# A third of eight ff pairs by seven products in the second product, with sums of one piece a row

## The chip, the cores and the metric

The kernel runs on one core of a Trainium2 chip. The metric is device time in microseconds; the median of three runs of the kernel before is 1011.67 us (1010.93 to 1014.6).

## The reference

A gated linear scan over 6080 time steps of 2 sequences with 256 channels gives 12160 tokens; each then passes a feed-forward layer of 2048 hidden units with a gate of its own:

```python
sig = 1.0 / (1.0 + np.exp(-f_logit))
f = lower_bound + (1.0 - lower_bound) * sig
for t in range(S):
    h = f[:, t] * h + (1.0 - f)[:, t] * x[:, t]
    y[:, t] = h
h = y.reshape(B * S, D) @ w_in            # 12160 x 256 by 256 x 2048
g = h * np.clip(h + 3.0, 0.0, 6.0) / 6.0
out = (g @ w_out).astype(np.float32)      # by 2048 x 256
```

## The kernel before

**Tiles.** Channels, hidden units and outputs lie on the partitions, tokens along the rows. Tokens are cut into 24 runs (`token_runs`): 20 of 512 columns and 4 of 480, alternately of sequence 0 and 1. The 2048 hidden units are 16 ff blocks of 128. Every float32 operand is split into a high part (rounded to the matmul's format, on ACT) and a low part (the rest, on DVE), and a product of two blocks is three matmuls: high by high, high by low, low by high. `split` is this pair of instructions (lines 406 to 415).

**Stages.** The first four runs are computed directly (`direct`, line 575). From then on runs go in ten pairs. `prep_pair` loads the gate input (`ft`) and x (`xt`) of both runs, scans them and builds the operands of the first product; sums of operands are made by DMAs that POOL issues and that add into their destination (`add_into`, line 246). For each of 8 pairs of ff blocks, `quad` makes the 2 x 2 block product (two ff blocks by two token runs) with seven block products instead of eight (`seven`, matmuls on line 620) and applies the gate (`gate`: ACT line 481, DVE line 483).

**Second product.** For most ff pairs it is plain: `mm2`, eight block products of three matmuls (line 512). For the first GROUP = 2 ff pairs of a run pair, in nine of the ten run pairs, `chain` uses seven products here too. It needs seven operands, each split: b11, b21, b22 are gated blocks as they are, t1, t3, t2 and t4 are sums, made in place in w11 and w12 by four POOL DMAs. Both ff pairs lie in one buffer of two blocks a row, so one DMA or one split serves both. The weight sums are made once by `prep_s2`.

**What sets the order.** A planner (`ordered`) lists every instruction as a job with a cost, needs and a due time that comes from PE's own order, and writes the five engines' programs in the order it plans. Each engine then runs its program in that order and waits where something is not ready. In PE's order products of the quads alternate with a fill from `queue` (plain second products and the steps of `chain`); FILLS says how many. `Ring` is a set of buffers used in turn; a new use waits for all users of the old one. `SCRATCH` is the space in SBUF, per partition, where descriptors of POOL's DMAs are kept. Buffers are placed `[P, 2, BANK]`: with 480 columns the second block begins 32 columns behind the end of the first.

Of the kernel before, what the change touches and what calls it, by code (L numbers as in the profile page):

```python
# [20 lines left out]
GROUP = 2  # L21
FILLS = ((2, 3, 3),) * 7 + ((2, 2, 2),)
# [39 lines left out]
class Ring:  # L62


    def __init__(self, pool, name, n, shape, dtype):
        self.pool, self.name, self.n, self.shape, self.dtype = pool, name, n, shape, dtype
        self.made, self.last, self.left = 0, {}, None
# [42 lines left out]
SCRATCH = 1024  # L110
# [90 lines left out]
def gated_scan_then_ffn(  # L201
# [26 lines left out]
    zeros = const.tile([P, BANK], BF16, name="zeros")  # L228
# [20 lines left out]
    r_ft = Ring(work, "ft", 2, [P, KD, BANK], F32)  # L249
# [94 lines left out]
    def scan_x(h, pieces):  # L344
# [154 lines left out]
    def mm2(f, h, m, ghi, glo, done):  # L499
# [21 lines left out]
        second.setdefault((h, m), []).append(j)  # L521
        if len(second[h, m]) == (NF - 2 * GROUP + 1 if seeded else NF):
# [346 lines left out]
```

## Time and profile before

| | |
|---|---|
| median of three runs | 1011.67 us |
| the profiled execution | 1010.72 us |
| its span, first to last instruction | 1008.9 us |
| PE busy | 989.6 us (98%), 4343 matmuls |
| DVE busy | 794.0 us (79%) |
| ACT busy | 698.4 us (69%) |
| POOL busy | 68.8 us (7%) |
| sums of second-product operands by DMA | 28 of 512 KB, 8 of 480 KB |
| sums of first-product operands by DMA | 32 of 256 KB, 8 of 240 KB |
| stores | 48 |

The busy time of PE counts matmuls that overlap, so it tells where PE stood, not how fast it was. The chain of waits, the timeline of an engine with its idle time in brackets, and the single DMAs with their time to landing tell the rest.

### The profile page before, as it was taken

Reading aid. Unit: us, or ns where it says so; the run is one execution under the profiler, and the core shown is the slowest. Engines: PE = TensorE matmul, PEld = TensorE weight load, DVE = VectorE, ACT = ScalarE, POOL = GpSimd, SP = SyncE. Lnnn points to the kernel's source line nnn. Section 1 sums busy time; section 2 is a strip of 40 time slices with the busy share of each in tenths; the row PEclk is TensorE's granted clock in tenths of the full one; section 3 lists DMA queues with packets and bytes.
Section 4 is the critical chain, followed back from the end, with each engine's and each line's share of the span. In section 5 each row is a group of like instructions: output and inputs, shape, how many; then the busy total and the mean of one; then the engine's idle time right before and its main releaser. Section 6 shows DMA issues by size and latency. Waiting matters only on the chain. (4 is left out here: it accounts for less than half of the span.)

```text
span 1008.9 us, 11835 instructions
## 1 busy us (share of the span) xinstructions
PE 989.6 (98%) x4343; PEld 812.4 (81%) x4343; DVE 794.0 (79%) x1055; ACT 698.4 (69%) x1101; POOL 68.8 (7%) x80
## 2 busy tenths in 40 slices
PE   8999999999999999999999999999999999799998
PEld 3778888888887888888888888888888788688787
DVE  7997659889968869968968968986986885597763
ACT  7975666668677768668759668767777765676752
POOL 0000001000110110110110101001011011001100
PEclk9999999999999999999999999999999999899999
DMA  9750022021280261243135126017026123412401
GB/s 358 266 183 26 22 105 53 11 70 36 42 205 5 42 160 49 43 108 102 32 69 151 24 40 188 11 32 209 1 42 165 39 40 91 109 20 36 101 1 40
DMA packets 37866, 83.86 MB, mean 83 GB/s; under 512 B 3504, under 2 KB 11184, under 8 KB 37808
## 3 DMA queue, kind: packets, MB, share of 16 engines
q1 hardware_dynamic: 25424, 53.87, 15.5%
q0 software_dynamic: 11968, 28.97, 15.2%
q8 instruction: 34, 0.56, 0.2%
q10 hardware_dynamic: 416, 0.26, 0.1%
q14 instruction: 24, 0.20, 0.1%
HBM read 41.67 MB, written 12.45 MB: 54 GB/s over the span
## 5 line engine op out<-in xcount | busy, mean ns | idle before, releaser
L483 DVE SCALAR_TENSOR_TENSOR r<-r,bank 128x512 f32<-128x512 f32 (+1 forms) x304 | 204.2, 676 | 76.2 <-ACT r L481 75.4
L481 ACT ACTIVATE r<-bank 128x512 f32<-128x512 f32 (+1 forms) x304 | 179.1, 591 | 110.8 <-PE bank L620 81.0
L620 PE MATMUL bank<-xhi,wst 128*128 128x512 f32 (+1 forms) x640 | 235.8, 389 | 8.8 <-DVE bank L611 8.8
L512 PE MATMUL bank<-ghi,whi 128*128 128x512 f32 (+1 forms) x620 | 240.6, 388 | 0.0
L512 PE MATMUL bank<-glo,whi 128*128 128x512 f32 (+1 forms) x620 | 240.2, 387 | 0.0
L512 PE MATMUL bank<-ghi,wlo 128*128 128x512 f32 (+1 forms) x620 | 240.2, 387 | 0.0
L620 PEld LDWEIGHTS bank<-xhi,wst 128*128 128x128 f32 x640 | 120.6, 188 | 33.6 <-DVE bank L611 9.6
L412 DVE SCALAR_TENSOR_TENSOR glo<-r,ghi 128x1024 fp32r<-128x1024 f32 (+1 forms) x98 | 117.6, 1207 | 28.6 <-ACT ghi L406 27.9
L512 PEld LDWEIGHTS bank<-glo,whi 128*128 128x128 f32 x620 | 116.4, 188 | 23.5
L512 PEld LDWEIGHTS bank<-ghi,whi 128*128 128x128 f32 x620 | 116.4, 188 | 23.4 <-issue 0.2
L512 PEld LDWEIGHTS bank<-ghi,wlo 128*128 128x128 f32 x620 | 116.3, 188 | 23.2 <-DVE wlo L294 0.2
L415 DVE TENSOR_TENSOR glo<-r,ghi 128x1024 fp32r<-128x1024 f32 (+1 forms) x89 | 107.0, 1208 | 22.3 <-ACT ghi L408 21.8
L620 PE MATMUL bank<-xlo,wst 128*128 128x512 f32 (+1 forms) x320 | 124.2, 388 | 0.0
L406 ACT ACTIVATE ghi<-r 128x1024 fp32r<-128x1024 f32 (+1 forms) x98 | 102.4, 1047 | 31.1 <-PE bank L512 13.7
L408 ACT CAST ghi<-r 128x1024 fp32r<-128x1024 f32 (+1 forms) x89 | 91.9, 1040 | 34.1 <-PE bank L512 20.2
L611 DVE TENSOR_TENSOR bank<-bank,e 128x512 f32<-128x512 f32 (+1 forms) x80 | 55.3, 691 | 34.7 <-PE bank L620 28.4
L246 POOL DMA_DIRECT2D xt<-xt x40 | 34.7, 868 | 610.5 <-issue 233.9
L620 PEld LDWEIGHTS bank<-xlo,wst 128*128 128x128 f32 x320 | 60.3, 189 | 11.8
L481 ACT ACTIVATE r<-e 128x512 f32<-128x512 f32 (+1 forms) x80 | 49.7, 621 | 23.9 <-DVE e L609 23.6
L483 DVE SCALAR_TENSOR_TENSOR r<-r,e 128x512 f32<-128x512 f32 (+1 forms) x80 | 54.4, 680 | 13.8 <-ACT r L481 13.6
L620 PE MATMUL bank<-xlo,whi 128*128 128x512 f32 (+1 forms) x160 | 61.9, 387 | 0.0
L620 PE MATMUL bank<-xhi,whi 128*128 128x512 f32 (+1 forms) x160 | 61.9, 387 | 0.0
(94 smaller groups left out, 1387.5 us busy)
## 6 DMA issues: line engine op xcount, KB each, us to landing
r<-r POOLq DMA_DIRECT2D x28, 512.0 KB, 5.0
outT<-o SPq DMA_DIRECT2D x40, 256.0 KB, 2.4
ft<-fT SPq DMA_DIRECT2D x19, 512.0 KB, 5.2
xt<-xT SPq DMA_DIRECT2D x18, 512.0 KB, 5.8
xt<-xt POOLq DMA_DIRECT2D x32, 256.0 KB, 3.2
wst<-w SPq DMA_DIRECT2D x14, 512.0 KB, 3.9
wst<-w SPq DMA_DIRECT2D x14, 511.5 KB, 4.9
r<-r POOLq DMA_DIRECT2D x8, 480.0 KB, 4.8
```

The source lines that it names most:

```text
L246: return job("POOL", ISSUE_ADD, lambda: nc.gpsimd.dma_start(out=out(), in_=src(), accum_op=ALU.add), needs, bufs, moves=2 * size)
L406: nc.scalar.mul(to(hi), cut(src), -1.0)
L408: nc.scalar.copy(to(hi), cut(src))
L412: nc.vector.scalar_tensor_tensor(out=to(lo), in0=cut(src), scalar=-1.0, in1=to(hi).bitcast(F32), op0=ALU.mult, op1=ALU.subtract)
L415: nc.vector.tensor_tensor(to(lo), cut(src), to(hi).bitcast(F32), op=ALU.subtract)
L481: b = job("ACT", act_cost(n, psum=True), lambda: nc.scalar.activation(r.get()[:, i, :n], src.get()[:, :n], AF.Relu, bias=3.0, scale=-1.0 i ...
L483: return job("DVE", dve_cost(n), lambda: nc.vector.scalar_tensor_tensor(out=r.get()[:, i, :n], in0=r.get()[:, i, :n], scalar=6.0, in1=src. ...
L512: nc.tensor.matmul(bank.get()[:, :n], wt[f][:, D + m * P:D + (m + 1) * P], g.get()[:, half, :n], start=(start and i == 0), stop=(stop and ...
L611: nc.vector.tensor_tensor(o, x, y, op=ALU.add)
L620: nc.tensor.matmul(bank.get()[:, :n], wt(), x(), start=(start and z == 0 and i == 0), stop=(z == len(parts) - 1 and i == 2), skip_group_ch ...
```

## The change

- **Third ff pair.** GROUP becomes 3, in PARTS of two and one: ff pairs 0 and 1 share buffers of two blocks a row, ff pair 2 has its own of one block (`r_r1`). `chain` makes every sum and every split once for each part, so four DMA sums become eight, of 512 KB and 256 KB in runs of 512 columns. A chain step is nine matmuls instead of six. FILLS is rebalanced, and the chain enters the queue one quad later.
- **Blocks close together.** Blocks lie `n` columns apart (`piece`), so a sum over two 480-column blocks is one stretch of 960 a row instead of two of 480.
- **Room.** `ft` has one buffer instead of two; outputs leave from `r` buffers 0 and 1 (6 and 7 for the first runs) instead of buffers of their own; weight sums go into columns of `whi` and `wlo` whose old content has been read, one into `spare_w`, which also serves as the zeros of the start; SCRATCH is 512 instead of 1024.
- **Weight sums.** `prep_s2` runs per ff pair, and ahead of the second run pair instead of the first.

```diff
@@ -18,8 +18,9 @@
 P = 128
 BANK = 512
 LAG = 4
-GROUP = 2
-FILLS = ((2, 3, 3),) * 7 + ((2, 2, 2),)
+PARTS = ((0, 1), (2,))
+GROUP = sum(map(len, PARTS))
+FILLS = ((2, 3, 2),) * 3 + ((2, 3, 3),)*5
...
@@ -107,7 +109,9 @@
 ISSUE = 480
 ISSUE_ADD = 1000
 DIRECT = 4
-SCRATCH = 1024
+FT = 1
+EARLY_AT = {(2, 1): 7, (1, 0): 6, (2, 0): 5}
+SCRATCH = 512
...
-    zeros = const.tile([P, BANK], BF16, name="zeros")
+    spare_w = const.tile([P, 2, P], F32R, name="spare_w")
...
-    r_ft = Ring(work, "ft", 2, [P, KD, BANK], F32)
+    r_ft = Ring(work, "ft", FT, [P, KD, BANK], F32)
...
-    r_r = Ring(work, "r", 8, [P, 2, BANK], F32)
-    r_o = Ring(work, "o", 2, [P, BANK], F32)
+    r_r = Ring(work, "r", 8, [P, 2 * BANK], F32)
+    r_r1 = Ring(work, "r1", 4, [P, BANK], F32)
+    r_ec = Ring(work, "ec", 1, [P, BANK], F32)
     r_e = Ring(work, "e", 2, [P, BANK], F32)
-    r_ghi = Ring(work, "ghi", 4, [P, 2, BANK], F32R)
-    r_glo = Ring(work, "glo", 4, [P, 2, BANK], F32R)
+    r_ghi = Ring(work, "ghi", 4, [P, 2 * BANK], F32R)
+    r_glo = Ring(work, "glo", 4, [P, 2 * BANK], F32R)
...
-        u, t, s = r_ft.new(), r_ft.new(), r_wst.new()
+        u, t = [r_r.at(k, shape=[P, KD, BANK]) for k in (4, 5)]
+        s = r_wst.new()
...
-        ft, xt = r_ft.new(), r_r.at(7) if h == 2 else r_xt.new()
+        ft, xt = [r_r.at(EARLY_AT[h, k], shape=[P, KD, BANK]) if (h, k) in EARLY_AT else r.new()
+                  for k, r in enumerate((r_ft, r_xt))]
...
+    def piece(b, i, n):
+        return b.get()[:, i * n:(i + 1) * n]
...
-    def split_both(n, r, needs, flip):
+    def split_flat(n, r, needs, flip):
+
+        if r.shape[1] == BANK:
+            (ghi, k), (glo, _) = r_ghi.half(), r_glo.half()
+            return [((ghi, k), (glo, k))], split(r, ghi, glo, lambda b: b.get()[:, :n], n, needs, flip, lambda b: piece(b, k, n))
         ghi, glo = r_ghi.new(), r_glo.new()
-        return ghi, glo, split(r, ghi, glo, lambda b: b.get()[:, :, :n], 2 * n, needs, flip)
+        return [((ghi, k), (glo, k)) for k in range(2)], split(r, ghi, glo, lambda b: b.get()[:, :2 * n], 2 * n, needs, flip)
...
-        ot = r_r.at(2 * (h % 2) + m) if h >= len(runs) - 2 else r_o.new()
-        cut = lambda: ot.get()[:, 0, :n] if h >= len(runs) - 2 else ot.get()[:, :n]
+        if h not in outs:
+            outs[h] = r_r.at(h % 2 if h >= DIRECT else 6 + h % 2)
+        ot = outs[h]
+        cut = lambda: piece(ot, m, n)
...
-            if not p:
-                raws[h] = [r_r.at(4 + k) for k in range(4)]
-            outs = [(x, p) for x in raws[h]]
+            part = next(part for part in PARTS if p in part)
+            if p == part[0]:
+                raws.setdefault(h, []).append([r_r.at(4 + k) if len(part) == 2 else r_r1.at(k) for k in range(4)])
+            outs = [(x, p - part[0]) for x in raws[h][-1]]
...
+        for j in range(4):
+            k = 4 * p + j
+            if k < NF // 2:
+                f = 2 * k + 1
+                out = [wt[f][:, :P] for wt in (whi, wlo)]
+                free = [*first_reads[f], *s_done[k]]
+            elif k < NF // 2 + GROUP:
+                f = 2 * (k - NF // 2)
+                out = [wt[f][:, D + P:] for wt in (whi, wlo)]
+                free = [*reads[f, 1], *(adds if f == 2 * p else s2_adds[f // 2])]
+            else:
+                assert k == NF // 2 + GROUP
+                out, free = [spare_w[:, i, :] for i in range(2)], []
+            hi = job("ACT", act_cost(P), lambda j=j, out=out: nc.scalar.copy(out[0], sv(j)), [*done, *free], [t])
+            lo = job("DVE", dve_cost(P), lambda j=j, out=out: nc.vector.tensor_tensor(
+                out[1], sv(j), out[0].bitcast(F32), op=ALU.subtract), [hi], [t])
+            s2_out[p, j], s2_done[p, j] = out, [hi, lo]
...
+        r_ghi.left = r_glo.left = None
         made = g_done[h]
-        g11, g12, g21, g22 = [[m[k] for m in made] for k in range(4)]
-        both = lambda b: b.get()[:, :, :n]
+        flat = lambda b: b.get()[:, :(b.shape[1] // BANK) * n]
 
         def sum_into(out, x, needs):
-            return add_into(4 * GROUP * n * P, lambda: both(out), lambda: both(x), needs, [out, x])
+            return add_into(4 * (out.shape[1] // BANK) * n * P, lambda: flat(out), lambda: flat(x), needs, [out, x])
         ops = {}
-        ops["b11"] = split_both(n, w11, g11, True)
-        t1 = sum_into(w11, w12, [*g12, *ops["b11"][2]])
-        ops["t1"] = split_both(n, w11, [t1], False)
-        t3 = sum_into(w12, w22, [*g22, t1])
-        t2 = sum_into(w11, w22, [*g22, *ops["t1"][2]])
-        ops["t2"] = split_both(n, w11, [t2], True)
-        ops["b21"] = split_both(n, w21, g21, False)
-        ops["b22"] = split_both(n, w22, g22, True)
-        ops["t3"] = split_both(n, w12, [t3], True)
-        t4 = sum_into(w11, w21, [*g21, *ops["t2"][2]])
-        ops["t4"] = split_both(n, w11, [t4], False)
+
+        def operand(name, w, z, needs, flip):
+            pieces, done = split_flat(n, w[z], needs[z], flip)
+            ops.setdefault(name, []).extend((g, done) for g in pieces)
+            return done
+        w11, w12, w21, w22 = [[part[k] for part in raws[h]] for k in range(4)]
+        g11, g12, g21, g22 = [[[made[p][k] for p in part] for part in PARTS] for k in range(4)]
+        every = range(len(PARTS))
+        d11 = [operand("b11", w11, z, g11, True) for z in every]
+        t1 = [[sum_into(w11[z], w12[z], [*g12[z], *d11[z]])] for z in every]
+        dt1 = [operand("t1", w11, z, t1, False) for z in every]
+        t3 = [[sum_into(w12[z], w22[z], [*g22[z], *t1[z]])] for z in every]
+        t2 = [[sum_into(w11[z], w22[z], [*g22[z], *dt1[z]])] for z in every]
+        dt2 = [operand("t2", w11, z, t2, True) for z in every]
+        for z in every:
+            operand("b21", w21, z, g21, False)
+        for z in every:
+            operand("b22", w22, z, g22, True)
+        for z in every:
+            operand("t3", w12, z, t3, True)
+        t4 = [[sum_into(w11[z], w21[z], [*g21[z], *dt2[z]])] for z in every]
+        for z in every:
+            operand("t4", w11, z, t4, False)
 
...
-    prep_s2()
     for h, h2 in pairs[1:]:
         prep_pair(h, h2)
     before = iter(())
     for h, h2 in pairs:
         group = GROUP if h > DIRECT else 0
+        if h == DIRECT + 2:
+            for p in range(GROUP):
+                prep_s2(p)
```

On POOL, one run pair in the middle of the program; `r4` is w11, `r5` w12, `r6` w21, `r7` w22, and the `xt` rows are the next pair's first-product sums. Before:

```order
L246 DMA r4_2893<-r5_2922 128x1024
L246 DMA r5_2922<-r7_2961 128x1024
L246 DMA r4_2893<-r7_2961 128x1024
L246 DMA r4_2893<-r6_2956 128x1024
L246 DMA xt1_3141<-xt0_3167 128x512
L246 DMA xt0_3167<-xt0_3167 128x512
L246 DMA xt1_3141<-xt0_3167 128x512
L246 DMA xt1_3141<-xt1_3141 128x512
```

And now, where `r10` to `r13` are the same four blocks of the third ff pair:

```order
L250 DMA r4_2918<-r5_2988 128x1024
L250 DMA r5_2988<-r7_3006 128x1024
L250 DMA r10_3068<-r11_3091 128x512
L250 DMA r11_3091<-r13_3109 128x512
L250 DMA r4_2918<-r7_3006 128x1024
L250 DMA r10_3068<-r13_3109 128x512
L250 DMA r4_2918<-r6_3018 128x1024
L250 DMA r10_3068<-r12_3128 128x512
L250 DMA xt1_3144<-xt0_3212 128x512
L250 DMA xt0_3212<-xt0_3212 128x512
L250 DMA xt1_3144<-xt0_3212 128x512
L250 DMA xt1_3144<-xt1_3144 128x512
```

Each sum is followed by its counterpart for the third ff pair; t2 (`r4<-r7`) has four sums ahead of it instead of two, and t2' (`r10<-r13`) follows it directly.

On ACT, around the split of t2 (`ghi<-r4`) in the same run pair. Before:

```order
L599 ACTIVATE e1_3103<-bank0_0_3092 128x512
L481 ACTIVATE r1_3068<-bank6_0_3006 128x512
L550 ACTIVATE o0_3113<-bank3_0_2600 128x512
L406 ACTIVATE ghi0_3121<-r4_2893 128x1024
L601 COPY bank4_0_3128<-bank5_0_3105 128x512
L406 ACTIVATE ghi2_3139<-r7_2961 128x1024
L481 ACTIVATE r2_3149<-bank7_0_3096 128x512
L601 COPY o1_3156<-bank2_0_3130 128x512
```

And now:

```order
L616 ACTIVATE e0_3221<-bank0_0_3208 128x512
L413 ACTIVATE ghi3_3226<-r4_2918 128x1024
L491 ACTIVATE r3_3192<-bank1_0_3104 128x512
L413 ACTIVATE ghi0_3180<-r10_3068 128x512
L413 ACTIVATE ghi2_3246<-r7_3006 128x1024
L618 COPY ec0_3251<-bank2_0_3182 128x512
L491 ACTIVATE r1_3258<-bank0_0_3208 128x512
L491 ACTIVATE r0_3271<-bank7_0_3214 128x512
L491 ACTIVATE r2_3154<-e1_3121 128x512
L401 ACTIVATE last_67<-xt1_3144 128x1
```

The split of t2' (`ghi0<-r10`) stands two rows behind that of t2, and ahead of the split of b22 (`ghi2<-r7`), the copy out of a bank (`ec0`) and the gates of the quad in work.

On SP, the stores of the run pair before and the loads of the next, same place. Before:

```order
L552 DMA outT<-o1_3034 128x512
L552 DMA outT<-o0_3057 128x512
L552 DMA outT<-o1_3078 128x512
L242 DMA ft0_3119<-fT 128x2x512
L552 DMA outT<-o0_3113 128x512
L242 DMA xt1_3141<-xT 128x2x512
L242 DMA ft1_3143<-fT 128x2x512
L242 DMA xt0_3167<-xT 128x2x512
```

And now:

```order
L569 DMA outT<-r0_3077 128x512
L569 DMA outT<-r1_3101 128x512
L246 DMA ft0_3123<-fT 128x2x512
L569 DMA outT<-r0_3077 128x512
L246 DMA xt1_3144<-xT 128x2x512
L569 DMA outT<-r1_3101 128x512
L246 DMA xt0_3212<-xT 128x2x512
L246 DMA ft0_3414<-fT 128x2x512
```

The second load of `ft` moved behind all others; in the program it stands 118 matmuls behind the last load ahead of it (7 in the order before).

## Rows read from the trace of the kernel before

**Rows 1.** The page's busy line: us, share of the span, instructions.
```profile
PE 989.6 (98%) x4343; PEld 812.4 (81%) x4343; DVE 794.0 (79%) x1055; ACT 698.4 (69%) x1101; POOL 68.8 (7%) x80
```
**Rows 2.** The chain of waits in order of time: start us, us, what.
```profile
803.02 2.04 PE bank L512 x9
...
989.70 15.62 PE bank L512 x72
```
**Rows 3.** Timeline of PE at its gaps: start us, us, instruction, idle before it.
```profile
309.05 0.47 PE L620 MATMUL bank<-ghi,whi 128*128 128x512 f32 x1 [0.67 <-ACT ghi L406]
...
790.49 0.50 PE L620 MATMUL bank<-xhi,wst 128*128 128x512 f32 x1 [2.15 <-DVE bank L611]
...
866.73 0.77 PE L620 MATMUL bank<-xhi,wst 128*128 128x480 f32 x1 [6.64 <-DVE bank L611]
867.29 0.60 PE L620 MATMUL bank<-xlo,wst 128*128 128x480 f32 x1
...
870.87 0.39 PE L620 MATMUL bank<-glo,whi 128*128 128x480 f32 x1
...
947.31 0.49 PE L620 MATMUL bank<-ghi,whi 128*128 128x480 f32 x1 [1.07 <-ACT bank L601]
```
**Rows 4.** Timeline of ACT where it waits longest for a sum.
```profile
787.52 1.99 ACT L408 CAST ghi<-r 128x1024 fp32r<-128x1024 f32 x2 [3.13 <-DMA r<-r]
...
863.90 1.00 ACT L406 ACTIVATE ghi<-r 128x960 fp32r<-128x960 f32 x1 [7.75 <-DMA r<-r]
...
945.79 1.00 ACT L406 ACTIVATE ghi<-r 128x960 fp32r<-128x960 f32 x1 [3.03 <-DMA r<-r]
```
**Rows 5.** Groups by line: count, busy us, mean ns, idle before; the chain's matmuls.
```profile
L620 PE MATMUL bank<-ghi,whi 128*128 128x512 f32 (+1 forms) x126 | 49.4, 392 | 1.7 <-ACT bank L601 1.1 <-ACT ghi L406 0.7
```
**Rows 6.** Groups by line: splits of one block on ACT and DVE.
```profile
L565 DVE TENSOR_TENSOR glo<-r,ghi 128x512 fp32r<-128x512 f32 x62 | 42.5, 687 | 12.4 <-ACT ghi L564 12.2
L564 ACT CAST ghi<-r 128x512 fp32r<-128x512 f32 x62 | 38.2, 617 | 21.9 <-DVE r L483 21.8
```
**Rows 7.** Timeline of DVE: the low part of t1's split in three run pairs.
```profile
686.30 1.23 DVE L415 TENSOR_TENSOR glo<-r,ghi 128x1024 fp32r<-128x1024 f32 x1 [0.19 <-ACT ghi L408]
...
849.22 1.16 DVE L415 TENSOR_TENSOR glo<-r,ghi 128x960 fp32r<-128x960 f32 x1 [0.32 <-ACT ghi L408]
...
935.18 1.16 DVE L415 TENSOR_TENSOR glo<-r,ghi 128x960 fp32r<-128x960 f32 x1 [0.58 <-ACT ghi L408]
```
**Rows 8.** DMA issues of the whole span: KB each, median us to landing.
```profile
ft<-fT SPq DMA_DIRECT2D x19, 512.0 KB, 5.2
```
**Rows 9.** Single DMAs issued at 685.69, 687.93, 731.92, 848.86, 853.94, 934.80: us to landing.
```profile
r<-r POOLq DMA_DIRECT2D x1, 512.0 KB, 4.4
r<-r POOLq DMA_DIRECT2D x1, 512.0 KB, 5.3
...
xt<-xt POOLq DMA_DIRECT2D x1, 256.0 KB, 3.2
...
r<-r POOLq DMA_DIRECT2D x1, 480.0 KB, 4.7
r<-r POOLq DMA_DIRECT2D x1, 480.0 KB, 9.9
...
r<-r POOLq DMA_DIRECT2D x1, 480.0 KB, 5.9
```
**Rows 10.** Timeline of POOL: t3 and t2 of three run pairs.
```profile
685.69 0.86 POOL L246 DMA_DIRECT2D r<-r  x1 [4.19 <-DVE r L483]
687.93 0.86 POOL L246 DMA_DIRECT2D r<-r  x1 [1.39 <-DVE glo L415]
...
848.86 1.22 POOL L246 DMA_DIRECT2D r<-r  x1 [4.25 <-issue]
853.94 1.20 POOL L246 DMA_DIRECT2D r<-r  x1 [3.86 <-DVE e L609]
...
934.80 1.21 POOL L246 DMA_DIRECT2D r<-r  x1 [4.23 <-DVE bank L611]
941.02 1.20 POOL L246 DMA_DIRECT2D r<-r  x1 [5.01 <-DVE r L483]
```

More of the change, by code (lines that the diff above doesn't have):

```diff
@@ L66, in __init__ @@
         self.pool, self.name, self.n, self.shape, self.dtype = pool, name, n, shape, dtype
-        self.made, self.last, self.left = 0, {}, None
+        self.made, self.last, self.left, self.halves = 0, {}, None, 0
     def new(self):
@@ L71, in new, with half, at @@
         return self.at((self.made - 1) % self.n)
-    def half(self):
+    def half(self, most=None):
         left, self.left = self.left, None
         if left is None:
-            self.left = self.new()
+            self.left = self.new() if most is None else self.at(self.halves % most)
+            self.halves += 1
             return self.left, 0
         return left, 1
-    def at(self, k, dtype=None):
-        self.last[k] = Buf(self.pool, f"{self.name}{k}", self.shape, dtype or self.dtype, self.last.get(k))
+    def at(self, k, dtype=None, shape=None):
+        self.last[k] = Buf(self.pool, f"{self.name}{k}", shape or self.shape, dtype or self.dtype, self.last.get(k))
         return self.last[k]
@@ L508, in emit @@
                 r, half = ghi
-                nc.tensor.matmul(bank.get()[:, :n], w_whole[f, 1][2](m), r.get()[:, half, :n], start=start, stop=stop)
+                nc.tensor.matmul(bank.get()[:, :n], w_whole[f, 1][2](m), piece(r, half, n), start=start, stop=stop)
                 return
@@ L512, in emit @@
                 nc.tensor.matmul(
-                    bank.get()[:, :n], wt[f][:, D + m * P:D + (m + 1) * P], g.get()[:, half, :n],
+                    bank.get()[:, :n], wt[f][:, D + m * P:D + (m + 1) * P], piece(g, half, n),
                     start=(start and i == 0), stop=(stop and i == 2), skip_group_check=seeded,
@@ L694, in quad @@
         for r, (i, j), tiles in ((x, (0, 3), ((f, h), (f2, h2))), (y, (1, 2), ((f, h2), (f2, h)))):
-            ghi, glo, cl = split_both(n, r, [done[i], done[j]], r is x)
-            todo += [(fz, hz, ((ghi, k), (glo, k), cl)) for k, (fz, hz) in enumerate(tiles)]
+            pieces, cl = split_flat(n, r, [done[i], done[j]], r is x)
+            todo += [(fz, hz, (*g, cl)) for g, (fz, hz) in zip(pieces, tiles)]
         if p < NF // 2 - 1:
@@ L726, in prep_s2 @@
         for j, x, y, op in todo:
-            done.append(job("DVE", dve_cost(GROUP * P), lambda j=j, x=x, y=y, op=op: nc.vector.tensor_tensor(
+            done.append(job("DVE", dve_cost(P), lambda j=j, x=x, y=y, op=op: nc.vector.tensor_tensor(
                 sv(j), x(), y(), op=op), [*adds, *done], [u, t]))
-        for k in range(4 * GROUP):
-            f = 2 * k + 1
-            part = lambda k=k: flat(t)[:, k * P:(k + 1) * P]
-            free = [*done, *first_reads[f], *s_done[k]]
-            hi = job("ACT", act_cost(P), lambda f=f, part=part: nc.scalar.copy(whi[f][:, :P], part()), free, [t])
-            lo = job("DVE", dve_cost(P), lambda f=f, part=part: nc.vector.tensor_tensor(
-                wlo[f][:, :P], part(), whi[f][:, :P].bitcast(F32), op=ALU.subtract), [hi], [t])
-            s2_done.extend([hi, lo])
+        for j in range(4):
[15 more added lines that the diff above has]
+            s2_out[p, j], s2_done[p, j] = out, [hi, lo]
@@ L767, in one @@
                     wdone = w_done[f, 1]
                 else:
[L769 to L771 removed]
+                    key = p, int(wname[1]) - 1
+                    ws, wdone = [lambda w=w: w for w in s2_out[key]], s2_done[key]
@@ L772, in one @@
+                xs = [lambda b=b, k=k: piece(b, k, n) for b in (hi, lo)]
+                parts.append((ws, wdone, [], xs, done, [hi, lo]))
             return product(n, bank, parts, needs, start)
@@ L782, in step @@
             if not steps:
-                steps.append(seven(n, (o11, o12, o21), (o22, r_o.new()), one, then, False))
+                steps.append(seven(n, (o11, o12, o21), (o22, r_ec.new()), one, then, False))
             next(steps[0], None)
```

46 lines of the change are left out of this document (22 added, 24 removed).

## The prediction

> **What bounds the kernel now.** The busy line of the page was read first: the tensor engine (PE) is busy 98% of the span, VectorE (DVE) 79%, ScalarE (ACT) 69% [rows 1]. So time is the number of matmuls times their pitch, plus the places where PE stands. The chain of waits gives the pitch: nine matmuls of 512 columns take 2.04 us, 0.2267 each, and 72 of 480 columns take 15.62 us, 0.2169 each [rows 2]. (The 388 ns of a matmul in the line groups overlap with the next one and price nothing.) Then the timeline of PE was searched for gaps in the steady part: 0.67, 2.15, 6.64 and 1.07 us [rows 3]. After the longest the granted clock was low for a while: from 866.73 to 870.87 ten matmuls took 4.14 us, where ten of 0.2169 take 2.17; that is 2.0 us more. Sum of gaps and clock: 0.67 + 2.15 + 6.64 + 1.07 + 2.0 = 12.5 us.
>
> All these gaps stand where the seven products of the second product wait for a sum made by DMA. ACT stood 3.13, 7.75 and 3.03 us for such a sum just before the last three [rows 4], and PE then stood 2.15, 6.64 and 1.07 us: ACT's wait less 1.0 to 2.0 us of cover. So the second thing that sets the time is how late a sum lands.
>
> **Part 1, matmuls.** Seven products for eight save one block product of three matmuls in each pair of token runs that uses them. Today 126 matmuls of the kind ghi,whi are 9 pairs by 14 [rows 5]; the new order has 9 by 21 of them, and 9 by 8 fewer of the plain kind. Net it is 9 x 3 = 27 fewer. Seven pairs have 512 columns, two 480: 21 x 0.2267 + 6 x 0.2169 = **6.1 us less**, all of it on PE.
>
> **Part 2, more splitting.** The third ff pair now needs seven operands of one block instead of two of two blocks. One block costs ACT 0.617 and DVE 0.687 us [rows 6]; two blocks about 1.0 on ACT [rows 4] and 1.2 on DVE [rows 7]. ACT: 7 x 0.617 - 2 x 1.0 = +2.3; DVE: 7 x 0.687 - 2 x 1.2 = +2.4 us per pair, some 21 us each over nine pairs. Spread over a span of 1008.9 us that lifts DVE from 79 to about 81% [rows 1]; it lies beside PE's work and I cost it at nothing. The twelve weight sums in place of eight add a few us to DVE once, ahead of their first use. If the cover is gone, the price is in part 4.
>
> **Part 3, buffers.** Outputs go through r0 and r1, the buffers of the later quads. In the program's order the last store of r1 stands 48 matmuls (10.9 us) ahead of the gate that writes r1 again; stores are short and I take nothing. With one ft buffer instead of two, the second load of ft waits for the first one's scan, and on SP's queue nothing but the next pair's stores stands behind it. From this load to the first matmul that needs its sum stand 85 matmuls, 19.3 us (203 before). Between lie a load of 5.2 us [rows 8], a sum of 3.2 us [rows 9] and eight ACT and DVE instructions, an estimate of 8 us at about 1 us each [rows 4, 6, 7]: 16.4 us, so some 3 us are spare and I take nothing.
>
> **Part 4, eight DMA sums instead of four, and half the descriptor space.** This decides. Per pair POOL now issues t1, t3, t2, t4; after the change each is two sums, one of 512 KB (two blocks) and one of 256 KB, in the order t1, t3, t1', t3', t2, t2', t4, t4'. The diff also halves SCRATCH, from 1024 to 512 bytes.
>
> What the trace shows of that space: in a pair with 512 columns t3 was issued at 685.69 and took 4.4 us to land, until 690.1; t2 was issued at 687.93, 2.2 us after t3 and while it was in flight [rows 9, 10], 0.4 us after the split of t1 was done (686.30 + 1.23) [rows 7]. In both pairs with 480 columns the split of t1 was done at 850.38 and 936.34 [rows 7], but t2 went out only at 853.94 and 941.02 [rows 10]. What had just happened is that t3 had landed: 848.86 + 4.7 = 853.56 and 934.80 + 5.9 = 940.70 [rows 9, 10]. So there POOL could not have two sums in flight, and the difference is that a sum of 480 columns has two pieces a row, 256 pieces for 128. I take it that 1024 bytes hold two sums of 128 pieces but not two of 256. Then 512 bytes hold one sum of 128 pieces and not two: making the sums one piece a row and halving the space leaves the 480-column pairs where they are and puts all other pairs into the same state. (The Trainium skill, DMA: Bandwidth & Descriptors, section "SWDGE vs HWDGE vs iDMA", says that GpSimd's transfers are written as descriptors into rings in SBUF; it gives no limit for a full ring, so it changes no number here.)
>
> What it costs, for a pair with 512 columns, in us from the start of t1 in the order, with landings of 4.4 to 5.3 for 512 KB and 3.2 to 4.2 for 256 KB (lone: 3.2; the upper end scaled by 5.3/4.4 and a little for the loads) [rows 9], 0.35 from a landing to the next issue where space is awaited [rows 9, 10] and, my choice, 0.3 more where the data is. The order leaves t1' at 7.5, t3' at 10.2, t2 at 14.1, t2' at 15.6; t2's split stands on ACT at 20.9, 6.8 us after its issue. One at a time: t1 at 0.5, t3 at 5.5, landing at 9.9; t1' 10.3 to 13.5 (14.5); t3' 14.1 (15.1) to 17.4 (19.3); t2 at 17.7 (19.6), that is 3.6 to 5.5 late, landing at 22.1 (24.9). ACT waits 1.2 to 4.0 for it. After split and gate it comes to t2' 1.65 us later; t2' was issued 0.35 after t2's landing and takes 3.2 to 4.2: another 1.9 to 2.9. **ACT waits 3.1 to 6.9 us**. Less the cover of 1.0 to 2.0, PE stands 1.1 to 5.9 us per pair. Behind the waiting split on ACT are the split of b22, the copy that frees the bank and three gates, on which the next quad's matmuls wait, so little of it is made good later. I take the middle, 3.5 us, which is nearest to the mean of what the two 480-column pairs show for one sum at a time, 6.64 (with loads of the next pair in flight; its t2 took 9.9 us) and 1.07 (without) [rows 3, 9]: 3.9. Nine pairs: **+31.5 us** (10 to 53). The stalls of today, 12.5, are replaced by these and go.
>
> The Trainium skill (DMA: Bandwidth & Descriptors, "Anatomy of one DMA") gives a GpSimd transfer as about 2.0 us plus its bytes at 436 GB/s: an estimate of 2.6 us for 256 KB and 3.2 for 512. By it the three sums that stand in a row would land some 2.5 us earlier and a pair would cost about 1 us, in all 1002. The trace shows 3.2 and 4.4 to 5.3 [rows 9], so the rows are used.
>
> **Sum.** The profiled execution took 1010.7 us, its span 1008.9; the median of the runs is 0.95 above the first. 1010.7 - 6.1 - 12.5 + 31.5 = 1023.6; with 0.95, **1025 us**.
>
> **The rivals.** (a) Sums are not held apart: 512 bytes hold two sums of 128 pieces. Then t2 and t2' land as early as t2 does today, the 480-column pairs lose their delay too (one piece a row), and stalls vanish: 1011.7 - 6.1 - 12.5 = 993, or 1006 if as much stands as today. For it: nothing in the trace shows the size of the space itself. Against: two of two 480-column pairs. It decides as soon as two sums of 128 pieces fit in 512 bytes. (b) They are held apart, but landings are at the short end and the cover at the long end: 1.1 us x 9 = 10: 1003; from 1.5 to 2.6 us a pair it is no change that can be measured. (c) Held apart, and t2 meets the next pair's loads in every pair as it did at 853.94: 8 x (6.64 + 2.0) + 1.07 = 70: 1063. Against: with one ft buffer only three of four loads come then. (d) The late ft load stalls the next pair's first quad, if the work before it takes over 19.3 us; at 1 to 2 us on top in nine pairs 1034 to 1043, within the upper end. That the change does not remove matmuls is excluded by the order.
>
> **How the numbers follow.** A measurement of this kernel tells about 0.5%, 5.1 us, from no change: 1006.6 and 1016.7. Held apart with 2.6 us or more a pair: 0.60. With 1.5 to 2.6 us (no change): 0.16. With less: 0.08, the other part of (b). (a): 0.12. (c): 0.04. Faster 0.20, same 0.16, slower 0.64. The range leaves out most of (a) and (c): 1000 to 1048.
>
> **What would show it.** In the profile after: matmuls 27 fewer; POOL's sums t2 and t2' each issued 0.3 to 0.4 us after the sum before landed, in 512-column pairs too; ACT waits of 3 to 7 us for a sum once a pair, and PE gaps behind them, nine times. If t2' goes out about 1.6 us after t2, part 4 is wrong and (a) holds; if it is held but PE shows no gaps, the cover was larger than the three rows say.

## The result, and the profile after

The changed kernel takes 1024.5 us (median, 1024.3 to 1026.3), the kernel before, timed beside it, 1011.35; the ratio is 1.0127 with a 95% interval of 1.0103 to 1.0151. The forecast was 1025 us and slower, in a range of 1000 to 1048.

The busy line of the page, to lay beside [rows 1]:

```profile
PE 995.7 (97%) x4315; PEld 803.8 (79%) x4316; DVE 811.6 (79%) x1114; ACT 704.7 (69%) x1150; POOL 98.2 (10%) x116
```

PE runs 28 matmul records less (27 matmuls, and one record that the trace has not) and is "busy" 6.1 us longer. That is the mark of many short waits: a record of 0.39 us overlaps its neighbours at a pitch of 0.2267, so a wait under about 0.16 us, and that much of every longer one, counts as busy. From here on the loss of a kernel is therefore taken from starts: for each matmul record from 160 us on, the time since the start of the one before, less the pitch (0.2267 us, 0.2169 from about 845 us on, where the runs have 480 columns [rows 2]), added up over the span. (The runs of 480 and of 512 columns overlap there for a while, so a loss depends by up to 0.7 us on where the pitch is switched.) One pair shows that it holds: before, from t1 of one pair (439.91) to the next (520.15) stand 354 matmuls, by 0.2267 80.25 us, and the time is 80.24; after, from 444.10 to 527.23, stand 351, 79.57 us, and the time is 83.13: 3.56 us lost in that pair.

| | before | after |
|---|---|---|
| span of the profiled execution, us | 1008.9 | 1022.5 |
| loss of PE from 160 us on, us | 14.0 | 36.2 |
| number of matmuls (records) | 4343 | 4315 |
| ACT waiting for sums of the second product, us | 20.9 | 57.4 |

The span grew by 13.6 us: 22.1 more loss, 6.1 less by the matmuls left out, and 2.4 less that is left over for the first 160 us. (With the pitch taken from each matmul's own columns the losses are 14.2 and 35.7, and 1.8 is left over.) Most of that last term is one gap of before that is gone after:

```profile
60.52 0.73 PE L575 MATMUL bank<-xhi,whi 128*128 128x512 f32 x2 [1.51 <-DVE r L483]
```

Where the loss comes from shows on POOL. The timeline of the eight sums of one pair with 512 columns (start us, us, instruction, idle before it), in the order t1, t3, t1', t3', t2, t2', t4, t4':

```profile
444.10 0.86 POOL L250 DMA_DIRECT2D r<-r  x1 [12.01 <-DVE r L493]
449.17 0.89 POOL L250 DMA_DIRECT2D r<-r  x1 [4.21 <-DMA r<-r]
454.11 0.87 POOL L250 DMA_DIRECT2D r<-r  x1 [4.05 <-DVE r L493]
458.45 0.89 POOL L250 DMA_DIRECT2D r<-r  x1 [3.47 <-DMA r<-r]
462.46 0.87 POOL L250 DMA_DIRECT2D r<-r  x1 [3.12 <-DVE glo L422]
467.90 0.89 POOL L250 DMA_DIRECT2D r<-r  x1 [4.57 <-DVE bank L628]
471.46 0.87 POOL L250 DMA_DIRECT2D r<-r  x1 [2.67 <-DMA r<-r]
476.19 0.88 POOL L250 DMA_DIRECT2D r<-r  x1 [3.86 <-DVE glo L419]
```

And the landings of t1', t3', t2 and t2' (issued at 454.11, 458.45, 462.46 and 467.90; KB, us to landing):

```profile
r<-r POOLq DMA_DIRECT2D x1, 256.0 KB, 3.7
r<-r POOLq DMA_DIRECT2D x1, 256.0 KB, 3.7
r<-r POOLq DMA_DIRECT2D x1, 512.0 KB, 5.1
r<-r POOLq DMA_DIRECT2D x1, 256.0 KB, 3.2
```

458.45 + 3.7 = 462.15, and t2 goes out at 462.46; 462.46 + 5.1 = 467.6, and t2' goes out at 467.90. Five of the seven sums that follow t1 stand 0.3 us behind the landing of the one before, whatever the releaser in brackets says; t3 and t3', which wait for t1 and t1' in the program itself, stand 0.6 us behind (454.11 + 3.7 = 457.81, and t3' goes out at 458.45). In the whole span no DMA of POOL is issued while another one is in flight. Before, t2 went out while t3 was in flight in pairs with 512 columns, and 0.3 to 0.4 us behind its landing in the others [rows 9, 10]. Now all pairs look like the two with 480 columns.

ACT (first fence: splits of t1', t2, t2' in the same pair) and then PE (second fence) wait for it:

```profile
457.83 0.62 ACT L415 CAST ghi<-r 128x512 fp32r<-128x512 f32 x1 [1.69 <-DMA r<-r]
467.61 1.06 ACT L413 ACTIVATE ghi<-r 128x1024 fp32r<-128x1024 f32 x1 [2.20 <-DMA r<-r]
471.17 1.58 ACT L413 ACTIVATE ghi<-r 128x512 fp32r<-128x512 f32 x2 [2.01 <-DMA r<-r]
```

```profile
471.85 0.50 PE L637 MATMUL bank<-ghi,whi 128*128 128x512 f32 x1 [0.45 <-ACT ghi L413]
472.58 0.51 PE L637 MATMUL bank<-glo,whi 128*128 128x512 f32 x1 [0.23 <-DVE glo L419]
474.49 0.50 PE L637 MATMUL bank<-xhi,wst 128*128 128x512 f32 x1 [0.35 <-DVE r L493]
476.93 0.47 PE L637 MATMUL bank<-ghi,whi 128*128 128x512 f32 x1 [0.77 <-DVE bank L628]
```

Unlike the one long gap of [rows 3], there are several short ones, and the last two do not name a split. The copy of a bank, the gates and the DVE additions stand behind the late splits in their engines' orders; that they pass the delay on is read from this order. In one of the two pairs with 480 columns PE stood 2.24 us at a stretch (until 880.58), and then the granted clock was low, as after the gap of 6.64 before: 0.57 on the mean of 4 us, that is mostly the lower of its two levels (1.2 and 2.4 GHz). The stretch (its length, then PE, PEld, DVE, ACT and POOL busy, granted clock, DMA share, GB/s):

```profile
880.00:884.00 4.00, 3.42 (x10) 2.81 (x11) 3.79 (x5) 3.33 (x6) 0.63 (x1) 0.57 0.93 234
```

### The profile page after: what moved, and what is told of

It reads as the page before. It is cut to its first block, busy times and chain, and to the rows that moved or that the text cites. A ratio compares the mean times of both kernels' runs of the same rounds, so it can differ in the third digit from the quotient of the medians.

```text
span 1022.5 us, 12064 instructions
## 1 busy us (share of the span) xinstructions
PE 995.7 (97%) x4315; PEld 803.8 (79%) x4316; DVE 811.6 (79%) x1114; ACT 704.7 (69%) x1150; POOL 98.2 (10%) x116
## 4 chain that ended last, share of the span: by engine, by line
PE 77%; issue 9%; DMA 5%; DVE 3%; ACT 3%; POOL 2%; POOLq 0%; ACTq 0%; DVEq 0%
PE bank L526 35%; PE bank L637 33%; PE bank L592 8%; DMA r<-r 5%; POOL r L250 2%; DVE glo L419 1%; ACT r L491 1%; ACT ghi L413 1%; PE bank L602 1%; DVE glo L422 1%; DVE e L626 1%; DVE bank L628 0%; DVE r L493 0%; ACT ec L618 0%; ACT r L567 0%
## 5 line engine op out<-in xcount | busy, mean ns | idle before, releaser
L526 PE MATMUL bank<-ghi,whi 128*128 128x512 f32 (+1 forms) x548 | 212.8, 388 | 0.0
L526 PE MATMUL bank<-glo,whi 128*128 128x512 f32 (+1 forms) x548 | 212.5, 388 | 0.0
L526 PE MATMUL bank<-ghi,wlo 128*128 128x512 f32 (+1 forms) x548 | 212.4, 388 | 0.0
L419 DVE SCALAR_TENSOR_TENSOR glo<-r,ghi 128x1024 fp32r<-128x1024 f32 (+3 forms) x125 | 131.0, 1054 | 44.0 <-ACT ghi L413 44.0
L422 DVE TENSOR_TENSOR glo<-r,ghi 128x1024 fp32r<-128x1024 f32 (+3 forms) x107 | 114.5, 1071 | 40.5 <-ACT ghi L415 40.4
L413 ACT ACTIVATE ghi<-r 128x1024 fp32r<-128x1024 f32 (+3 forms) x125 | 112.8, 920 | 47.3 <-DMA r<-r 34.9
L415 ACT CAST ghi<-r 128x1024 fp32r<-128x1024 f32 (+3 forms) x107 | 98.8, 928 | 40.5 <-DMA r<-r 22.5
L526 PEld LDWEIGHTS bank<-ghi,whi 128*128 128x128 f32 x548 | 102.9, 188 | 20.7 <-issue 0.2
L526 PEld LDWEIGHTS bank<-glo,whi 128*128 128x128 f32 x548 | 102.8, 188 | 20.7
L250 POOL DMA_DIRECT2D r<-r x72 | 62.9, 874 | 345.1 <-DVE r L493 154.3
L637 PE MATMUL bank<-ghi,whi 128*128 128x512 f32 (+1 forms) x180 | 70.8, 393 | 7.6 <-DVE bank L628 6.2
L637 PE MATMUL bank<-glo,whi 128*128 128x512 f32 (+1 forms) x180 | 70.9, 394 | 2.0 <-DVE glo L419 1.8
L628 DVE TENSOR_TENSOR bank<-bank,e 128x512 f32<-128x512 f32 (+1 forms) x80 | 55.0, 687 | 21.9 <-PE bank L637 18.8
L637 PE MATMUL bank<-ghi,wlo 128*128 128x512 f32 (+1 forms) x180 | 69.7, 387 | 0.0
```

Source lines behind the costliest of these rows:

```text
L250: return job("POOL", ISSUE_ADD, lambda: nc.gpsimd.dma_start(out=out(), in_=src(), accum_op=ALU.add), needs, bufs, moves=2 * size)
L413: nc.scalar.mul(to(hi), cut(src), -1.0)
L415: nc.scalar.copy(to(hi), cut(src))
L419: nc.vector.scalar_tensor_tensor(out=to(lo), in0=cut(src), scalar=-1.0, in1=to(hi).bitcast(F32), op0=ALU.mult, op1=ALU.subtract)
L422: nc.vector.tensor_tensor(to(lo), cut(src), to(hi).bitcast(F32), op=ALU.subtract)
L526: nc.tensor.matmul(bank.get()[:, :n], wt[f][:, D + m * P:D + (m + 1) * P], piece(g, half, n), start=(start and i == 0), stop=(stop and i = ...
```

## Experiments

The theory is that of part 4 of the prediction: sums leave one at a time because the descriptor space holds no second one, and the late sums are the loss. The rivals are that the splits of the third ff pair, the single ft buffer and the buffers for outputs make PE wait, or that the DMA engines take the sums one after the other in any case.

### 64 bytes more

```diff
-SCRATCH = 512
+SCRATCH = 576
```

> The changed kernel with one number different: SCRATCH 576 instead of 512; nothing else moves. Theory (too little descriptor space holds POOL's sums apart): a sum of one piece a row for 128 rows is what a DMA of POOL takes out of the space, and 512 bytes hold one such sum but not two, while 1024 held two. If the limit lies just above 512, then t2' goes out 1.5 to 2 us after t2, t1' no longer waits for t3's landing, ACT's waits for t2 and t2' (1.3 to 2.9 and 2.0 to 2.5 us in the changed kernel) shrink to below 1 us, and the time falls from 1024.5 to 995 to 1005 us. If the theory holds but 576 bytes are still too few, nothing changes at all: 1024 to 1026, and the gaps stay where they are. Rival (the splits of the third ff pair and the single ft buffer make PE wait, or the DMA engines take one sum after the other anyway): sums go out earlier but land as late as now, or land earlier and PE stands as long: 1019 to 1026.

Measured: 998.1 us (997.8 to 998.5), ratio to before 0.9870 (0.9849 to 0.9891), loss 8.7 us. Every engine runs the same instructions in the same order as in the changed kernel, and 64 bytes a partition are worth 26 us. The timeline of POOL in one pair (t3, t1', then t3' and t2 in one row, t2', t4, t4'), and the landing of t3' (issued at 372.58):

```profile
363.75 0.88 POOL L250 DMA_DIRECT2D r<-r  x1 [4.32 <-DMA r<-r]
366.05 0.87 POOL L250 DMA_DIRECT2D r<-r  x1 [1.42 <-DVE r L493]
372.58 1.78 POOL L250 DMA_DIRECT2D r<-r  x2 [5.67 <-DVE glo L422]
376.45 0.88 POOL L250 DMA_DIRECT2D r<-r  x1 [2.09 <-issue]
383.42 0.87 POOL L250 DMA_DIRECT2D r<-r  x1 [6.09 <-DVE glo L419]
385.52 0.88 POOL L250 DMA_DIRECT2D r<-r  x1 [1.23 <-DVE glo L419]
```

```profile
r<-r POOLq DMA_DIRECT2D x1, 256.0 KB, 3.6
```

t1' leaves 2.3 us after t3 and while it is in flight; t3' and t2 leave together. The third one, t2', leaves at 376.45, 0.3 us after t3' has landed (372.58 + 3.6 = 376.2) and with t2 still in flight: now two sums fit and a third waits. So the limit for two sums of 128 pieces lies above 512 and at or below 576 bytes, and it is the same for 256 and 512 KB. (Whether 1024 bytes would hold a third one, no run shows: there never were three.) The rival that splits and buffers cost the 36 us is out for three quarters of them. In its details the expectation missed: t2' left 3.0 to 4.8 us after t2 and not 1.5 to 2, and ACT's waits fell less than expected, for t2 to 0.4 to 2.0 us and for t2' to at most 1.5 (they were 0.9 to 2.9 and 1.5 to 2.5 in the changed kernel).

What sharing costs is seen here as well, but not in this pair, where t2 took 7.5 us and t2' 7.3 (5.2 and 3.2 in the changed kernel): a load of 512 KB was in flight beside both, from 374.03 to 381.32. In the last pair, with only a store beside them, t2 (480 KB) took 6.0 us and t2' (240 KB) 4.5, against 4.3 and 3.2 one at a time in the changed kernel. With 576 bytes the sums land earlier all the same: the row from t1's issue to the landing of t4' takes 31.1 us on the mean of nine pairs, 35.6 in the changed kernel.

### Two ff pairs, blocks close together, with both sizes of the space

```diff
-    r_r = Ring(work, "r", 8, [P, 2, BANK], F32)
+    r_r = Ring(work, "r", 8, [P, 2 * BANK], F32)
...
+    def flat(b, n):
+        return b.get()[:, :2 * n]
...
-        both = lambda b: b.get()[:, :, :n]
+        both = lambda b: flat(b, n)
```

(and, in the second kernel, SCRATCH 512 for 1024).

> The kernel before (two ff pairs by seven products, SCRATCH 1024) with one thing of the change: blocks of r lie n columns apart, so a sum of two 480-column blocks is one piece a row. Theory (two pieces a row fill the space): in the two pairs with 480 columns t2 goes out before t3 has landed, as in the 512-column pairs; the PE gaps of 6.64 us (with about 2 us of low clock behind it) and 1.07 us go, all else stays: 1011.5 less 8 to 10, 1002 to 1004 us. Rival (the late t2 of those pairs is due to the loads of the next pair or to the order, not to pieces): within 2 us of the kernel before.

Measured: 1000.0 us (997.6 to 1001.8), ratio 0.9887 (0.9861 to 0.9914), loss 1.2 us. The layout alone gives 11 us. t3 and t2 of a pair with 480 columns:

```profile
846.06 0.86 POOL L246 DMA_DIRECT2D r<-r  x1 [4.34 <-issue]
848.15 0.86 POOL L246 DMA_DIRECT2D r<-r  x1 [1.23 <-DVE glo L415]
```

t3 landed 4.2 us after its issue, at 850.3; t2 leaves 2.1 us after t3 and so before that, as in the pairs with 512 columns; in [rows 10] it was 5.1. The issue itself fell from 1.2 to 0.86 us. The gain is a little above the forecast of 8 to 10, because of the other two gaps of [rows 3] that of 0.67 us went as well and that of 2.15 became 1.31.

> The kernel before with the flat blocks and with SCRATCH 512. Theory (512 bytes hold one sum): t2 goes out 0.3 to 0.4 us after t3 has landed in all nine pairs, also in the seven with 512 columns, where it went out 2.2 us after t3 before. There it lands 2 to 2.5 us later, against 1.3 us of slack between landing and split in the pair at 687.93, so ACT waits 0.5 to 1.2 us for it and PE hardly stands; in the 480-column pairs t2 stays as late as it was and the gaps stay: 1008 to 1014 us, that is 5 to 10 more than the flat blocks with 1024 bytes. Rival (the space has no part in it): the same time as flat blocks with 1024 bytes, within 2 us, and t2 going out before t3 has landed.

Measured: 1009.3 us (1004.5 to 1011.7), ratio 0.9982 (0.9963 to 1.0000), loss 12.1 us. t3 and t2 of a pair with 512 columns, and what ACT then waited for t2:

```profile
366.03 0.86 POOL L246 DMA_DIRECT2D r<-r  x1 [4.20 <-DVE r L489]
370.77 0.89 POOL L246 DMA_DIRECT2D r<-r  x1 [3.88 <-DVE r L489]
```

```profile
376.87 1.06 ACT L406 ACTIVATE ghi<-r 128x1024 fp32r<-128x1024 f32 x1 [1.87 <-DMA r<-r]
...
863.12 1.00 ACT L406 ACTIVATE ghi<-r 128x960 fp32r<-128x960 f32 x1 [5.20 <-DMA r<-r]
```

t3 landed 4.4 us after its issue, at 370.46, and t2 left 0.3 later. ACT waited 1.8 to 3.1 us for t2 in six of the seven pairs with 512 columns (0.7 in the other), more than the 0.5 to 1.2 expected, since t2 took 4.9 to 7.0 us there and not 5.3. PE lost 5.7 us behind the wait at 863 and some 6 in all other places together. So half the space takes back 9 of the 11 us, in a kernel that has nothing else of the change.

### t3' behind t2'

```diff
         t2 = [[sum_into(w11[z], w22[z], [*g22[z], *dt1[z]])] for z in every]
+        t3[1][0].needs.append(t2[1][0])
```

> The changed kernel with SCRATCH still 512, and one sum moved in POOL's order: t3' goes out behind t2' instead of ahead of t2. Theory (sums go one at a time, and t2 and t2' are late because t3' stands ahead of them): counted from t1, t1' lands at 13.5 to 14.5, t2 then goes out when its data is there, at about 14.5 instead of 18.4, and t2' at about 19 instead of 23.8; ACT's waits for both fall below 1 us. t3', t4 and t4' come one after the other behind them and end about where they do now, so a wait for t4' of 1 us may stay: 998 to 1008 us. Rival (extra splits and buffers make PE wait): no gain, 1020 to 1026.

Measured: 1038.3 us (1036.9 to 1041.2), ratio 1.0271 (1.0244 to 1.0299), loss 49.9 us. Wrong for the theory as I had worked it out, and outside the rival's range as well. Splits of t1', t2', t4 and t4' on ACT in one pair:

```profile
379.56 0.62 ACT L415 CAST ghi<-r 128x512 fp32r<-128x512 f32 x1 [4.14 <-DMA r<-r]
389.61 0.63 ACT L413 ACTIVATE ghi<-r 128x512 fp32r<-128x512 f32 x1 [3.33 <-DMA r<-r]
...
397.92 1.05 ACT L415 CAST ghi<-r 128x1024 fp32r<-128x1024 f32 x1 [1.11 <-DMA r<-r]
401.52 0.62 ACT L415 CAST ghi<-r 128x512 fp32r<-128x512 f32 x1 [2.55 <-DMA r<-r]
```

The wait for t2 is gone, as expected; the one for t2' is not, it is 1.0 to 3.3 us where below 1 was expected. And eight sums one after the other make a row that another order does not shorten: from t1's issue to the landing of t4' it takes 33.9 to 37.4 us in the changed kernel (35.6 on the mean of nine pairs) and 34.3 to 38.5 here (36.5). ACT, no longer held at t2, comes to t4 and t4' earlier and waits there, 2 to 2.6 us for t4' in every pair, where I had costed "a wait of 1 us may stay". That fits with nothing having been gained. Of the 14 us that were lost, a part is that t1' met the next pair's loads in more pairs (6.7 us in this one and 7.1 in the pair at 534, where it took 3.4 and 3.3 before the move); the rest was not settled. The stretch from 372 to 380 by queue:

```profile
q1 hardware_dynamic: 1113, 2.12, 81.4%
q0 software_dynamic: 159, 0.26, 18.4%
issues: line engine op xcount, KB each, median us to landing
xt<-xT SPq DMA_DIRECT2D x2, 512.0 KB, 6.4
```

> The changed kernel with SCRATCH 576 and t3' behind t2' in POOL's order. With 512 bytes this order cost 14 us more than the changed kernel's: t3' then stood ahead of t4, and t4 and t4' came 1 to 2.5 us late. Theory (there it was the room for one sum alone that made the order matter; with room for two the sums are late only by sharing): t2 no longer shares with t3', and t3' and t4 may overlap: 994 to 1000 us, within 4 us of the kernel with 576 bytes alone. Rival (the order itself is bad, t4 and t4' are late with any room): 1005 us or more.

Measured: 997.1 us (996.1 to 998.2), ratio 0.9866 (0.9845 to 0.9887), loss 6.9 us. With room for two, the order that cost 14 us costs nothing; 998.1 and 997.1 are the same within what the two intervals tell. The order is not bad; it matters only while sums queue.

### The third ff pair's sums on VectorE

```diff
         def sum_into(out, x, needs):
+            if out.shape[1] == BANK:
+                return job("DVE", dve_cost(n), lambda: nc.vector.tensor_tensor(flat(out), flat(out), flat(x), op=ALU.add),
+                           needs, [out, x])
             return add_into(4 * (out.shape[1] // BANK) * n * P, lambda: flat(out), lambda: flat(x), needs, [out, x])
```

> The changed kernel with SCRATCH 512 as it was, and the four one-block sums of the third ff pair as adds on VectorE. Theory (in the changed kernel the eight sums of a pair go one at a time, and that alone costs the 36 us that its matmuls lose): four sums a pair are left, as in the flat kernel with 512 bytes, whose matmuls lost 12.1 us; with 6.1 us of matmuls less than that kernel's 1009.3: 1001 to 1006 us. Rival (splits and buffers of the third ff pair cost PE): 1012 or more.

Measured: 1000.6 us (1000.1 to 1001.7), ratio 0.9901 (0.9878 to 0.9924), loss 12.3 us. Just under the low end. That the loss is the flat kernel's 12.1 is chance, for 7.3 of it stand in one pair. There t2 left at 612.14, 0.3 us behind the landing of t3, beside two loads of 512 KB (612.09 and 612.82), and took 7.8 us. ACT and then PE:

```profile
619.97 1.06 ACT L413 ACTIVATE ghi<-r 128x1024 fp32r<-128x1024 f32 x1 [6.15 <-DMA r<-r]
```

```profile
622.50 0.79 PE L637 MATMUL bank<-xhi,wst 128*128 128x512 f32 x1 [4.55 <-ACT bank L616]
```

In the pair ahead of it, from t1 at 516.84 to the next at 601.35, stand 373 matmuls: by 0.2267 84.56 us, and the time is 84.52. So with four sums in place of eight a pair can do without any loss although it has all that the third ff pair brings (its splits, one ft, the outputs' buffers, four additions on VectorE): these cost PE nothing that can be seen.

> With SCRATCH 576 the kernel took 998.1 us, although it has 27 matmuls (6.1 us) fewer than the flat kernel of two ff pairs at 1000.0; its matmuls still lost 8.7 us against their pitch from 160 us on, the flat kernel's 1.2. Here the four one-block sums of the third ff pair are adds on VectorE (about 0.69 us each, 2.7 us a pair) instead of DMAs; SCRATCH 576. Theory (what is left of the loss comes from sums that share the DMA engines: t2 and t2' took 7.5 and 7.3 us in the pair at 358, t2 of the flat kernel 5.4): the loss falls to 1 to 3 us: 998.1 less 6 to 7, 990 to 994 us. Rival (it comes from the extra splits on ScalarE and VectorE or from the single ft buffer): VectorE gets more work still, the loss stays or grows: 998 to 1005 us.

Measured: 992.0 us (991.1 to 993.3), ratio 0.9816 (0.9797 to 0.9836), loss 3.4 us: the best version. Busy line, and the 36 additions in the groups by line:

```profile
PE 982.5 (99%) x4315; PEld 805.6 (81%) x4316; DVE 831.3 (84%) x1150; ACT 702.9 (71%) x1150; POOL 66.6 (7%) x80
```

```profile
L775 DVE TENSOR_TENSOR r<-r,r 128x512 f32<-128x512 f32 (+1 forms) x36 | 24.3, 681 | 0.7
```

It is faster than the kernel with 576 bytes alone by 6.1 us (5.3 of it is loss): that is what the four extra DMAs cost even where two fit. The loss of 3.4 is a little above the 1 to 3 that were expected.

### One ft buffer

```diff
-        ft, xt = r_ft.new(), r_r.at(7, ...
+        ft, xt = r_ft.at(0) if h >= DIRECT + 2 else r_ft.new(), r_r.at(7, ...
```

> The flat kernel of two ff pairs (SCRATCH 1024, 1000.0 us) with one buffer of ft instead of two for all run pairs from the second on, which moves one of the loads of ft in SP's order as the change did. Theory (the single ft buffer costs PE nothing): 998 to 1002 us. Rival (the late load of ft makes the next pair's first quad wait): 1 to 2 us in each of nine pairs, 1009 to 1018 us.

Measured: 996.2 us (996.1 to 996.3), ratio 0.9857 (0.9839 to 0.9875), no loss at all (-0.3, within the rounding of the pitch). A single ft buffer costs nothing here. It even comes out below the flat kernel's 1000.0; 1.5 us of that is the loss that went. It moves one load away from the sums, but the two kernels were not timed side by side and the flat one's times spread over 4 us, so I do not call a gain shown.

### More sums on VectorE

Both start from the kernel with the third ff pair's sums on VectorE; the first moves t2 of the first two ff pairs there too (576 bytes), the second all eight sums (512 bytes).

> The kernel with the third ff pair's sums on VectorE (992.0 us, 3.4 us of matmul loss left, ScalarE still waiting 1.1 to 2.3 us for t2 in five pairs), and t2 of the first two ff pairs on VectorE too: about 1.2 us more of it in each pair; POOL keeps t1, t3 and t4. Theory (what is left is the wait for t2's DMA): 988 to 991 us. Rival (VectorE, busy 84%, then makes the splits late and PE waits for it): 993 to 1000 us.

Measured: 1003.1 us (1001.0 to 1003.6), ratio 0.9921 (0.9906 to 0.9935), loss 13.6 us: slower than the rival's range. VectorE is busy 841.7 us, 10.4 more than in the best version, but only 3.4 us of PE's waits name its additions into banks (line 628), and 2.1 of these stand behind a late sum of POOL's: t1, issued at 443.51, 0.3 to 1.4 us behind three loads of 512 KB, took 8.9 us. ACT and then PE:

```profile
452.48 1.05 ACT L415 CAST ghi<-r 128x1024 fp32r<-128x1024 f32 x1 [3.63 <-DMA r<-r]
```

```profile
455.45 0.50 PE L637 MATMUL bank<-xhi,wst 128*128 128x512 f32 x1 [2.11 <-DVE bank L628]
```

Most of the rest of the loss is in waits too short to be named. What causes it is open; that it is VectorE's work is not shown.

> The changed kernel (SCRATCH 512) with all eight sums of the second product as adds on VectorE, none by POOL: 2.7 us a pair for the one-block sums and about 4.8 us for the two-block ones, 68 us in all, which lifts VectorE from 79 to about 86%. Theory (the whole loss of the changed kernel comes from how POOL's sums go out and land, and not from its splits and buffers): with no such sum the space does not matter, and the matmuls lose less than 5 us: 988 to 996 us. Rival (a share of the 36 us comes from splits, one ft buffer and outputs leaving from r buffers; VectorE's added work makes that worse): 1005 us or more.

Measured: 1010.8 us (1010.2 to 1011.8), ratio 1.0001 (0.9992 to 1.0011), loss 22.4 us, the rival's side. PE's longest waits in this kernel (us in total, times, longest):

```profile
PE bank L637 <- DVE bank L628: 9.5, 13, 1.1
PE bank L637 <- ACT bank L616: 4.6, 7, 0.7
```

PE waits for VectorE's additions into banks (a step of the seven products) and for bank copies on ACT, and for no sum of the second product by POOL, since there is none. This run therefore does not tell how much of the 36 us came from sums; it tells that PE waits for VectorE when that is busy 86% on average, long before it is full.

The kernels were timed in three sets, with the kernel before in each (1010.9, 1011.1 and 1010.7 us); differences of 1 or 2 us between sets are not clear of noise.

| kernel | us | loss, us |
|---|---|---|
| before | 1011.4 | 14.0 |
| changed | 1024.5 | 36.2 |
| changed, 576 bytes | 998.1 | 8.7 |
| changed, t3' late, 512 / 576 | 1038.3 / 997.1 | 49.9 / 6.9 |
| before, flat, 1024 / 512 | 1000.0 / 1009.3 | 1.2 / 12.1 |
| before, flat, one ft | 996.2 | -0.3 |
| third ff pair's sums on VectorE, 512 / 576 | 1000.6 / 992.0 | 12.3 / 3.4 |
| and t2 (576) / all sums (512) on VectorE | 1003.1 / 1010.8 | 13.6 / 22.4 |

## Why the prediction was right, point by point

**Matmuls** (part 1): 27 fewer, as forecast. That they are worth their 6.1 us shows between two kernels of the same loss: the profiled execution of the flat kernel with 512 bytes took 1008.3, that with the third ff pair's sums on VectorE and 512 bytes 1000.9, 7.4 less. Of this 1.5 is the beginning (the 655th matmul record starts at 161.60 in the one and at 160.07 in the other); 5.9 is left.

**Splits** (part 2) and **buffers** (part 3) were costed at nothing, and that held in the kernels with the third ff pair's sums on VectorE and in the one with a single ft buffer. The cover is not endless: with all sums on VectorE PE waited 9.5 us for its additions into banks.

**The space** (part 4): the mechanism was right, both halves of it. 1024 bytes hold two sums of 128 pieces but not two of 256, and 512 hold one. (That 512 hold one and not two, and that pieces count, is shown by the runs above; the number of bytes that a sum takes is not known closer than that.) The issue times came as worked out. By the working t2 goes out 17.2 to 19.1 us after t1 (17.7 and 19.6, each less 0.5) and t2' 21.9 to 24.8; in seven of the nine pairs it was 17.7 to 19.1 and 22.8 to 24.1, in the other two, where t1' took 5.7 and 6.7 us, up to 21.4 and 26.1.

**The size** was right in part by luck. ACT waited 3.4 to 4.8 us for t2 and t2' together (3.9 on the mean of nine pairs), at the low end of the forecast's 3.1 to 6.9. By the forecast's own cover of 1.0 to 2.0 us PE should have lost 1.9 to 2.9 a pair; it lost 4.0 (36.2 in nine). Two things were left out: t1' was late too (ACT waited 1.4 to 4.6 us for it in every pair), and a late split hands its delay on through the copies, gates and additions behind it. The forecast's 3.5 is the middle of its range: 5.0 us of ACT's waiting less 1.5 of cover. Measured were 3.9 of waiting for t2 and t2' and 4.0 lost, as if there were no cover. So two terms, the wait taken too long and the cover taken from three single waits, were off in opposite directions and made up for each other. That the two things left out are what ate the cover is argued, not shown by a run. On the total, 36.2 stands for the forecast 31.5, 14.0 for the old 12.5, and the 2.4 us left over for the beginning, which were not foreseen, close the sum: 22.1 - 6.1 - 2.4 = 13.6 against the forecast 12.9.

**Rival (a)** was close: it "decides as soon as two sums of 128 pieces fit in 512 bytes". They fit in 576, and the time is then 998, inside the 993 to 1006 that it gave. **Rival (c)**, loads met in every pair, is not what happened, but a sum that meets loads does take longer: t1' took 6.7 us in the pair at 858, 3.3 to 3.8 in six others, and that pair has the largest loss, over 6 us, a part of it by the low clock at 880 to 884. The rule weighed in part 4 (the Trainium skill, DMA: Bandwidth & Descriptors, section "Anatomy of one DMA") would give the sums 2.6 and 3.2 us, an estimate from its figures; in the changed kernel, where all stand singly, the medians to landing were 3.3 us for 256 KB and 4.6 for 512 KB, so the rows were the right choice.

**What the change meant for the time.** The layout alone is worth 11 us (1011.4 to 1000.0). The third ff pair is worth 2 more with room for two sums (998.1, not clear of noise), and 8 with its sums on VectorE (992.0; 4 against the flat kernel with one ft buffer). The halved space, against one of 576 bytes, costs 26 (1024.5) and hid both.

## What to carry to other kernels

Where a DMA of POOL was issued long after its data was ready, 0.3 us after the landing of an earlier one, it was short of descriptor space here, and the releaser that the profile named meant nothing; count the pieces of each transfer against the space before halving it. Where these transfers queued one at a time, another order only moved the wait; room for a second, or taking some of them off the queue, did more. Four small additions a pair fitted on a busy VectorE, and every step beyond them lost time: move such work in steps and measure each. And two equal totals prove little: look in which pair each loss stands.

## What was not expected of the hardware

- The step is sharp: 64 bytes of descriptor space per partition (512 to 576) moved the time from 1024.5 to 998.1 us, with the same instructions in the same order.
- The space taken goes by pieces, not by bytes moved: a sum of 256 KB in 128 pieces held the next one back just as a sum of 512 KB in 128 pieces, while two sums of 480 KB in 256 pieces did not fit into the 1024 bytes that hold two of 512 KB in 128.
- Issuing a sum of 256 pieces took POOL 1.20 to 1.22 us [rows 10], one of 128 pieces 0.86 to 0.89, whether it moves 256 or 512 KB.
- Sums in flight together took longer (6.0 and 4.5 us, where one at a time they took 4.3 and 3.2, with no load beside them), yet with 576 bytes the row of eight ends 4.5 us earlier on the mean.
